# Batch 1's second product as seven Strassen products, and a reordered slot ahead of it

## The chip, the cores and the metric

The kernel runs on one core of one Trainium2 chip. The metric is the device time of one execution in microseconds: median of three runs 208.55 us (208.01 to 209.11). The profile is of one execution with a span of 207.0 us. TensorE multiplies, ScalarE does activations and copies out of PSUM, VectorE does elementwise work and copies, GpSimd copies in SBUF and issues the loads that cast to bf16, SyncE issues stores and DMA transposes.

## The reference, cut to what matters

B = H = 8, S = 512 tokens, NS = 32 states, D = 64; d_model = 512, d_ff = 2048.

```python
scores = x @ state^T / 8 ;  a  = softmax(scores)  ;  xread = a  @ state   # [B,H,512,64]
scores2 = state @ x^T / 8 ; a2 = softmax(scores2) ;  sread = a2 @ x       # [B,H,32,64]
y = concat(xread, sread, axis=2), heads merged to rows                    # [B*544, 512]
out = gelu_exact(y @ w_in) @ w_out                                        # [B*544, 512] f32
```

The first product of the MLP is not taken of xread itself. For each batch the kernel forms P = state x w_in (block-diagonal by head), and then h = a x P, so that attention read and first product are one.

## The kernel before, in words

All work is ordered by hand: each engine runs its instructions in the order in which the Python code issues them, and an instruction that waits holds back everything behind it on its engine or issue queue. Waits follow from data and from buffers. PSUM has four rotating tiles `ps_f` (tag "f") for first products, P chunks, transposes and scores, and four fixed banks `o0` to `o3` for outputs.

Work on a batch b goes through these pieces:

- `load_x(b)` (GpSimd queue, cast to bf16, two buffers), `rearr(b)` (GpSimd copies x into `x4`), `xtr_dma(b)` (SyncE: DMA transpose of `x4` to `xT`), `rearr_ones(b)` (GpSimd copies x into `xo`, with ones beside it for row sums).
- `state_prep` transposes states and sets them into the block-diagonal `sbd`.
- `scores(b, half)` on TensorE, exp on ScalarE (a table load before and after), `norm(b, half)` on VectorE, and `atr_dma(b)` (SyncE: DMA transpose of `a` to `AT`); batches 0 and 1 use TensorE (`atr`) for that.
- `p_mm` makes one of four chunks of P in two PSUM tiles; `p_copy` copies one tile on ScalarE and one on VectorE. `pmat`, `burst` and `p_run` call them, with different PSUM banks.
- `M(k)` is first product number k: batch k // 16, rows m = k % 16 of d_ff; two matmuls of 128x512 into a `ps_f` tile and a Gelu on ScalarE into `gs[b]`. It needs P and AT of its batch. M(32), for example, is the first of batch 2.
- The second product has two forms. In the direct form, `U(u)` (`mm2`) does four matmuls of 128x512 for batch u // 16; sixteen units make a batch (`mm2_m` is the same with another order), and `evac` copies each output tile on VectorE and stores it. In Strassen's form g and w_out are split two by two, and seven products `X(b, "3"), "6", "4", "5", "1", "2", "7"` of 16 matmuls of 128x256 each stand in for the eight of the direct form. They need sums of g blocks (`g_sum`, VectorE), sums of w_out blocks (`w_sums(0)` to `w_sums(4)`, VectorE, once), and combine on VectorE, ScalarE and GpSimd (`u` and `v`).
- `sread`, `sread_out`, `srt` collect the state reads of all batches; their MLP runs at the end (`mm1_sr`, `R`).

In the kernel before, batches 0 and 1 have their second product in the direct form and batches 2 to 7 in Strassen's. The code runs in slots. A slot of batch b in the steady loop (`for b in range(2, B)`, p = 0 to 7) holds M pairs of batch b, the last five products of batch b - 1 (p = 0 to 4: "45127"), and attention and P of batch b + 1; p = 6 and 7 hold X(b, "3") and X(b, "6"). The second slot (M(16) to M(31)) is written out: it holds U12 to U22, and U23 to U31 go into the slot of batch 2. The loads are issued in `load_rest` in the order w_out 1, w_in 2, w_out 2, w_in 3, w_out 3, states of batches 2 to 7, x of batch 2, x of batch 3; x of batch 4 is issued in the second slot. Before a later load, a one-element copy `hold` from a column of g keeps GpSimd's queue back until that Gelu has run.

Of the kernel before, what the change touches and what calls it, by code (L numbers as in the profile page):

```python
# [17 lines left out]
def kernel(  # L18
# [8 lines left out]
    nc = tc.nc  # L27
# [8 lines left out]
    SJ = S // 128  # L36
# [75 lines left out]
    def load_w_out(i):  # L112
        nc.gpsimd.dma_start(out=w_out_bf[:, 4 * i:4 * i + 4, :], in_=w_out_r[:, 4 * i:4 * i + 4, :])
# [18 lines left out]

    def load_rest():
        load_w_out(1)
        for f in range(2, FC):
            load_w_in(512 * f, 512 * f + 512)
            load_w_out(f)
        load_st(2, B)
        load_x(2)
        load_x(3)  # L140


    def keep_warm(n):
# [288 lines left out]

    def burst(chunks, b_read=None):
        done = []
        first = len(chunks) < 4 and b_read is not None
        if first:
            sread(b_read)
        for i, (b, f) in enumerate(chunks):  # L440
            done.append((b, f, p_mm(b, f, ftile if i < 2 else otile)))
        for x in done[:2]:
            p_copy(*x)
        if b_read is not None and not first:
            sread(b_read)
        for x in done[2:3]:
            p_copy(*x)
        if b_read is not None:
            sread_out(b_read)
        for x in done[3:]:  # L450
            p_copy(*x)


    def pmat00(h):
        if h == 0:
            Ps[0] = att.tile([128, 2, d_ff], BF16, name="P", tag="P")
# [42 lines left out]
    def mm2(b, q, j):  # L499
        if q == 0:  # L500
            ops[b, j] = otile([128, d_model], "op")
        ps = ops[b, j]
        for m in range(4 * q, 4 * q + 4):
            nc.tensor.matmul(  # L504
                ps,
                lhsT=gs[b][:, m, j * 128:(j + 1) * 128],
                rhs=w_out_bf[:, m, :],
                start=(m == 0),
                stop=(m == MC - 1),
            )  # L510
        if q == 3:
            rows = out_rows(b, j)
            evac(ps, [(rows, slice(0, 128), 0, d_model)])

    def mm1_sr(m):
        hp = ps_f.tile([128, B * NS], FP32, name="hps", tag="f")
# [276 lines left out]
            nc.vector.tensor_tensor(out=rs["o", 0][:, :NH], in0=ps, in1=rs["u"], op=add)  # L793
            r_out(0)

    def p_run(b, fs, banks):
        done = []
        for f, at in zip(fs, banks):
            it = iter(at or ())
            tiles = (lambda shape, name: otile(shape, name, next(it))) if at else ftile  # L800
            done.append((b, f, p_mm(b, f, tiles)))
        for x in done:
            p_copy(*x)


    def M(*ms):
# [3 lines left out]
    def U(*us):  # L810
        for u in us:
            mm2(u // 16, u % 16 // 4, u % 4)
# [71 lines left out]
    srt(0)  # L884
    U(4, 5)
    rearr_ones(1)
    U(6)
    pmat(0, 2)
    norm(1, 0)
# [4 lines left out]
    sread_out(1)  # L894
    M(10, 11)
    mm2_m(0, 8)
    mm2_m(0, 9)
    burst([(0, 3), (1, 0)])
    mm2_m(0, 10)
    atr(1)  # L900
    M(12, 13)
    srt(1)
    M(14, 15)
    mm2_m(0, 11)
    begin(2)
    rearr(2)
    xtr_dma(2)
    rearr_ones(2)
    U(12)
    burst([(1, 1), (1, 2)])  # L910
    U(13)
    state_prep(2, B)
    M(16, 17)
    U(14)
    M(18, 19)
    U(15)
    burst([(1, 3), (2, 0), (2, 1)])
    U(16)


    u = 17
    for p in range(2, 8):
        if p == 4:
            scores(2, 0)
            scores(2, 1)
            norm(2, 0)
            norm(2, 1)
        if p == 7:
            atr_dma(2)
        if p == 3:  # L930
            begin(3)
            rearr(3)
            xtr_dma(3)
            rearr_ones(3)
        M(16 + 2 * p, 17 + 2 * p)
        U(u)
        u += 1
        if p in (5, 7):
            pmat(2, 2 + p // 7)
        if p >= 3:  # L940
            w_sums(p - 3)
        if p == 2:
            nc.gpsimd.tensor_copy(out=hold, in_=gs[1][:, 4, 0:1])
            load_x(4)

    for b in range(2, B):
        nb = b + 1
        for p in range(8):
            k = 16 * b + 2 * p
            if p == 1 and nb < B:  # L950
                scores(nb, 0)
                scores(nb, 1)
            if p in (2, 3) and nb < B:
                norm(nb, p - 2)
            if p == 3 and nb + 1 < B:
                xtr_dma(nb + 1)
            if p == 5 and nb < B:
                atr_dma(nb)
            if p == 6 and nb < B:
                srt(b)  # L960
            if p == 7 and nb == B - 1:
                srt(nb)
            M(k, k + 1)
            if b == 2:
                for _ in range(2 if p < 4 else 1):
                    if u < 32:
                        U(u)
                        u += 1
            elif p < 5:
                if p == 0:  # L970
                    g_sum(b - 1, "5")
                X(b - 1, "45127"[p])
                if p < 3:
                    g_sum(b - 1, "127"[p])
            if nb == B and p < 4:
                for m in range(4 * p, 4 * p + 4):
                    mm1_sr(m)
            if p == 1 and nb < B:
                sread(b)
                sread_out(b)  # L980
            if p == 4 and nb == B - 1:
                sread(nb)
                sread_out(nb)
            if p == 0 and b + 3 < B:
                nc.gpsimd.tensor_copy(out=hold, in_=gs[b][:, 0, 0:1])  # L985
                load_x(b + 3)
            if p == 0 and nb + 1 < B:
                begin(nb + 1)
                rearr(nb + 1)
            if p == 2 and nb + 1 < B:  # L990
                rearr_ones(nb + 1)
            if nb == B:
                if p == 4:
                    r_homes()
                    r_sum("5")
                    r_sum("2")
                if p == 5:
                    g_sum(b, "6")
                    R("3")
                    r_sum("1")  # L1000
                    R("4")
                    r_sum("6")
                    r_sum("7")
                if p == 6:
# [59 lines left out]
```

The softmax here doesn't subtract the row's maximum and nothing guards it: scores larger than these inputs give would overflow.

## Time and profile before

| what | value |
|---|---|
| median of three runs | 208.55 us |
| span of the profiled run | 207.0 us |
| TensorE granted clock | 1.0 |
| L478 first products (M), 248 matmuls of 128x512 | 63.9 us busy |
| L504 and L531 direct second products, 96 and 32 matmuls of 128x512 | 379 ns each by their records |
| L586 Strassen products, 640 matmuls of 128x256 | 273 ns each by their records |
| L580 sums of g blocks, 30 | 39.8 us busy |
| HBM read and written | 17.30 and 8.91 MB |

Matmul records overlap, since matmuls are pipelined; to price a run of them, the distance between starts is what counts. A busy share says how much an engine works, not what the end waits for: for that the chain of waits and the timelines are read. In timelines the first column is the start and the second the length, both in us; brackets hold idle time and what ended it. "SPq" is SyncE's issue queue.

### The profile page before, as it was taken

To read this page: it belongs to the slowest core of one execution; us is meant where nothing else is said; L and a number is where in the kernel's file an instruction comes from. 1 tells how busy PE (TensorE), PEld (TensorE's weight loads), DVE (VectorE), ACT (ScalarE), POOL (GpSimd) and SP (SyncE) were. 2 spreads that over 40 slices of the span, in tenths; PEclk is the share of its full clock that TensorE was granted. 3 is DMA by queue.
4 is the path that set the end of the run, shared out by engine and by line. 5 is a ranking of instruction groups with operands and counts; after the bars stand their busy time and mean duration, and the time that the engine had idled before them with its cause. 6 is when DMAs were issued, how large, how long until landed. Compare 5 with 4: busy or idle time off the path is not lost.

```text
span 207.0 us, 4716 instructions
## 1 busy us (share of the span) xinstructions
PE 200.9 (97%) x1979; PEld 131.8 (64%) x1979; DVE 138.0 (67%) x219; ACT 133.0 (64%) x240; POOL 62.4 (30%) x69
## 2 busy tenths in 40 slices
PE   7889999998999999999999999999999999999994
PEld 6644444443444567756776677757775788778893
DVE  2942675766919857996599858765878452165883
ACT  3864675679794769576965877587757566744120
POOL 8955400755073005720677005600220002200000
PEclk9999999999999999999999999999999999999999
DMA  6999999689363916827492602560106001030125
GB/s 200 184 168 203 206 198 197 99 237 185 70 80 79 271 29 88 168 103 105 47 175 69 172 0 63 94 203 3 52 3 203 3 0 51 3 152 0 54 92 163
DMA packets 40261, 23.14 MB, mean 112 GB/s; under 512 B 21808, under 2 KB 38320, under 8 KB 40240
## 3 DMA queue, kind: packets, MB, share of 16 engines
q0 software_dynamic: 13936, 8.10, 28.6%
q1 hardware_dynamic: 25616, 14.36, 26.9%
q10 hardware_dynamic: 688, 0.39, 0.6%
q8 instruction: 15, 0.25, 0.5%
q14 instruction: 6, 0.05, 0.1%
HBM read 17.30 MB, written 8.91 MB: 127 GB/s over the span
## 4 chain that ended last, share of the span: by engine, by line
PE 89%; DMA 4%; ACT 3%; POOL 2%; issue 0%; DVE 0%; POOLq 0%; ACTq 0%
PE xp L586 34%; PE hp L478 26%; PE op L504 9%; PE p_ps L415 4%; DMA w_out_bf<-in_moe_w_out_dram 4%; PE op L531 4%; PE hps L518 3%; PE rp L762 3%; PE xp L692 2%; PE pt L324 1%; PE sr L378 1%; POOL w_in_bf L105 1%; POOL sbd L95 1%; ACT g L485 1%; ACT L485 1%; ACT L331 1%
## 5 line engine op out<-in xcount | busy, mean ns | idle before, releaser
L485 ACT ACTIVATE g<-hp 128x512 bf16<-128x512 f32 x124 | 67.5, 604 | 31.0 <-PE hp L478 26.0
L478 PE MATMUL hp<-AT,P 128*128 128x512 bf16 x248 | 63.9, 380 | 0.1
L586 PEld LDWEIGHTS <-gsum 128*128 128x128 bf16 x448 | 43.4, 98 | 11.3 <-issue 2.1
L580 DVE TENSOR_TENSOR gsum<-g 128x2048 bf16<-128x2048 bf16 x30 | 39.8, 1346 | 0.1
L478 PEld LDWEIGHTS <-P 128*128 128x128 bf16 x248 | 22.7, 98 | 19.0 <-issue 1.3
L586 PE MATMUL xp<-ws,gsum 128*128 128x256 bf16 x256 | 30.6, 273 | 0.0
L427 DVE CAST P<-p_ps 128x512 bf16<-128x512 f32 x31 | 20.0, 683 | 13.2 <-PE p_ps L415 13.2
L504 PE MATMUL op<-w_out_bf,g 128*128 128x512 bf16 x96 | 23.7, 379 | 0.0
L586 PE MATMUL xp<-ws,g 128*128 128x256 bf16 x192 | 22.9, 273 | 0.0
L586 PE MATMUL xp<-w_out_bf,gsum 128*128 128x256 bf16 x192 | 22.8, 273 | 0.0
L586 PEld LDWEIGHTS <-g 128*128 128x128 bf16 x192 | 18.8, 98 | 4.3
L426 ACT CAST P<-p_ps 128x512 bf16<-128x512 f32 x31 | 17.0, 605 | 7.0 <-PE p_ps L415 7.0
L635 POOL TENSOR_TENSOR u<-s,oh 128x512 f32<-128x512 f32 x5 | 6.3, 1265 | 48.6 <-ACT oh L632 48.6
L504 PEld LDWEIGHTS <-g 128*128 128x128 bf16 x96 | 9.1, 98 | 11.5 <-issue 1.1
L218 POOL COPY x<-xb 128x1024 bf16<-128x1024 bf16 x12 | 12.6, 1081 | 10.9 <-DMA xb<-in_x_dram 10.9
L228 POOL COPY xo<-xb 128x1024 bf16<-128x1024 bf16 x12 | 14.5, 1241 | 1.3 <-PE sr L378 1.3
L347 DVE TENSOR_TENSOR a<-e,ics 128x512 bf16<-128x512 bf16 x14 | 13.8, 987 | 0.5
L344 DVE TENSOR_REDUCE cs<-e 128x16 f32<-128x512 bf16 x14 | 9.5, 676 | 3.8 <-ACT e L331 3.8
L415 PE MATMUL p_ps<-w_in_bf,sbd 64*32 64x512 bf16 x248 | 10.7, 382 | 0.6 <-ACT g L485 0.5
L605 POOL TENSOR_TENSOR v<-q,oh 128x512 f32<-128x512 f32 x5 | 6.4, 1286 | 14.6 <-ACT oh L637 14.6
L629 DVE TENSOR_TENSOR s<-xp,s 128x512 f32<-128x512 f32 x5 | 3.5, 691 | 11.0 <-PE xp L586 11.0
L985 POOL COPY hold<-g 128x1 bf16<-128x1 bf16 x3 | 1.0, 331 | 31.0 <-ACT g L485 31.0
(111 smaller groups left out, 225.7 us busy)
## 6 DMA issues: line engine op xcount, KB each, us to landing
xb<-in_x_dram POOLq DMA_DIRECT2D x7, 512.0 KB, 7.0
out_dram<-oh SPq DMA_DIRECT2D x13, 256.0 KB, 2.6
out_dram<-osb SPq DMA_DIRECT2D x10, 256.0 KB, 3.3
out_dram<-oh SPq DMA_DIRECT2D x5, 512.0 KB, 2.7
w_out_bf<-in_moe_w_out_dram POOLq DMA_DIRECT2D x4, 512.0 KB, 12.4
w_in_bf<-in_moe_w_in_dram POOLq DMA_DIRECT2D x6, 256.0 KB, 12.6
x0f<-in_x_dram SPq DMA_DIRECT2D x3, 256.0 KB, 3.9
w_in_bf<-in_moe_w_in_dram POOLq DMA_DIRECT2D x4, 128.0 KB, 4.1
```

Of the source, the lines that this page charges most:

```text
L218: nc.gpsimd.tensor_copy(out=A.x4[:, :, :, 64 * t:64 * t + 64].rearrange("p j c d -> p c j d"), in_=src[:, t],)
L228: eng.tensor_copy(out=A.xo[:, :, :, 2 + 64 * t:66 + 64 * t].rearrange("p j c d -> p c j d"), in_=src[:, t],)
L344: nc.vector.reduce_sum(out=cs, in_=e4, axis=AX.X)
L347: nc.vector.tensor_tensor(out=A.a[:, :, hs].rearrange("p g (c n) -> p g c n", n=NS), in0=e4, in1=ics[:, :, :].to_broadcast((128, G, 2, NS) ...
L415: nc.tensor.matmul(ps[t][32 * c:32 * c + 32, :], lhsT=sbd[64 * t:64 * t + 64, b, c, 32 * t:32 * t + 32], rhs=w_in_bf[64 * t:64 * t + 64, c ...
L426: nc.scalar.copy(out=dst[:, 0, :], in_=ps[0])
L427: nc.vector.tensor_copy(out=dst[:, 1, :], in_=ps[1])
L478: nc.tensor.matmul(hp, lhsT=Ps[b][:, t, m * 128:(m + 1) * 128], rhs=atts[b].AT[:, :, t, :], start=(t == 0), stop=(t == 1),)
L485: nc.scalar.activation(out=gs[b][:, m, :], in_=hp, func=AF.Gelu)
L504: nc.tensor.matmul(ps, lhsT=gs[b][:, m, j * 128:(j + 1) * 128], rhs=w_out_bf[:, m, :], start=(m == 0), stop=(m == MC - 1),)
L580: nc.vector.tensor_tensor(out=t, in0=g_q(b, h0, k0), in1=g_q(b, h1, k1), op=op)
L586: nc.tensor.matmul(ps[:, j - js[0], :], lhsT=lhs[:, m, 128 * j:128 * j + 128], rhs=rhs[:, m, :], start=(first and j == js[0] and m == 0), ...
```

## The change

Batch 1 takes Strassen's form too: X(1, "3") and X(1, "6") stand in the second slot and the other five in the slot of batch 2, so the steady loop loses its special case for batch 2. The weight sums, which are now needed a slot earlier, move to the first and second slots. The second slot is reordered: M(16) on come earlier, U12 to U15 of batch 0 later. The state and x of batch 2 are loaded ahead of the last chunk of w_out; x of batch 3 and the states of batches 3 to 7 are loaded in the second slot, behind holds, x of batch 4 and 5 in the slot of batch 2. One chunk of P of batch 1 is copied by VectorE alone, `burst` goes, and the last output tile of batch 0 is stored in two halves. What it is for: fewer matmul columns on TensorE, which is busy nearly all the time, and work that fills the places where TensorE waited.

```diff
     def load_rest():
         load_w_out(1)
-        for f in range(2, FC):
-            load_w_in(512 * f, 512 * f + 512)
-            load_w_out(f)
-        load_st(2, B)
+        load_w_in(1024, 1536)
+        load_w_out(2)
+        load_w_in(1536, 2048)
+        load_st(2, 3)
         load_x(2)
-        load_x(3)
+        load_w_out(3)
...
         if q == 3:
             rows = out_rows(b, j)
-            evac(ps, [(rows, slice(0, 128), 0, d_model)])
+            h = d_model // 2 if j == SJ - 1 else d_model
+            evac(ps, [(rows[:, n:n + h], slice(0, 128), n, n + h) for n in range(0, d_model, h)])
...
+    def p_copy_v(b, f, ps):
+        for t in range(2):
+            nc.vector.tensor_copy(out=Ps[b][:, t, f * 512:(f + 1) * 512], in_=ps[t])
+
+    def hold_for(b, m):
+        nc.gpsimd.tensor_copy(out=hold, in_=gs[b][:, m, 0:1])
...
     rearr_ones(1)
+    w_sums(2)
     U(6)
...
     mm2_m(0, 8)
+    p_run(1, (0, 1), (None, None))
     mm2_m(0, 9)
-    burst([(0, 3), (1, 0)])
+    atr(1)
+    pmat(0, 3)
     mm2_m(0, 10)
-    atr(1)
+    M(16, 17)
+    srt(1)
     M(12, 13)
-    srt(1)
-    M(14, 15)
     mm2_m(0, 11)
     begin(2)
     rearr(2)
     xtr_dma(2)
+    M(14, 15)
+    state_prep(2, 3)
+    pmat(1, 2)
+    hold_for(0, 15)
     rearr_ones(2)
     U(12)
-    burst([(1, 1), (1, 2)])
+    w_sums(0)
+    M(18, 19)
+    hold_for(1, 3)
+    load_x(3)
+    load_st(3, B)
     U(13)
-    state_prep(2, B)
-    M(16, 17)
+    w_sums(1)
+    M(20, 21)
+    scores(2, 0)
+    scores(2, 1)
+    w_sums(3)
     U(14)
-    M(18, 19)
+    p_run(1, (3,), ((3, 0),), p_copy_v)
+    begin(3)
+    rearr(3)
+    xtr_dma(3)
+    rearr_ones(3)
+    M(22, 23)
+    norm(2, 0)
+    M(24, 25)
+    p_run(2, (0,), ((1, 3),))
     U(15)
-    burst([(1, 3), (2, 0), (2, 1)])
-    U(16)
...
-    for p in range(2, 8):
...
-        if p == 7:
-            atr_dma(2)
...
-        M(16 + 2 * p, 17 + 2 * p)
-        U(u)
...
+    norm(2, 1)
+    X(1, "3")
+    atr_dma(2)
+    g_sum(1, "6")
+    M(26, 27)
+    M(28, 29)
+    p_run(2, (1,), ((1, 2),))
+    state_prep(3, B)
+    M(30, 31)
+    X(1, "6")
...
             M(k, k + 1)
-            if b == 2:
-                for _ in range(2 if p < 4 else 1):
-                    if u < 32:
-                        U(u)
-                        u += 1
-            elif p < 5:
+            if b == 2 and p in (0, 3):
+                pmat(2, 2 + p // 3)
+            if b == 2 and p == 1:
+                w_sums(4)
+            if p < 5:
                 if p == 0:
                     g_sum(b - 1, "5")
                 X(b - 1, "45127"[p])
...
             if p == 0 and b + 3 < B:
-                nc.gpsimd.tensor_copy(out=hold, in_=gs[b][:, 0, 0:1])
-                load_x(b + 3)
+                hold_for(b, 0)
+                load_x(4 if b == 2 else b + 3)
+            if p == 6 and b == 2:
+                hold_for(b, 12)
+                load_x(5)
```

More of the change, by code (lines that the diff above doesn't have):

```diff
@@ L430, in pmat @@
         p_copy(b, f, p_mm(b, f, ftile))
[L435 to L451, printed above, removed]
     def pmat00(h):
@@ L794, in R, with p_run @@
             r_out(0)
-    def p_run(b, fs, banks):
+    def p_run(b, fs, banks, copy=None):
         done = []
@@ L802, in p_run @@
         for x in done:
-            p_copy(*x)
+            (copy or p_copy)(*x)
+    def p_copy_v(b, f, ps):
[3 more added lines that the diff above has]
+        nc.gpsimd.tensor_copy(out=hold, in_=gs[b][:, m, 0:1])
     def M(*ms):
@@ L907 @@
     xtr_dma(2)
+    M(14, 15)
+    state_prep(2, 3)
+    pmat(1, 2)
+    hold_for(0, 15)
     rearr_ones(2)
     U(12)
-    burst([(1, 1), (1, 2)])
-    U(13)
-    state_prep(2, B)
-    M(16, 17)
-    U(14)
-    M(18, 19)
-    U(15)
-    burst([(1, 3), (2, 0), (2, 1)])
-    U(16)
-    u = 17
-    for p in range(2, 8):
[L923 to L927, printed above, removed]
-        if p == 7:
-            atr_dma(2)
[L930 to L934, printed above, removed]
-        M(16 + 2 * p, 17 + 2 * p)
-        U(u)
-        u += 1
[L938 to L944, printed above, removed]
+    w_sums(0)
[3 more added lines that the diff above has]
+    load_st(3, B)
+    U(13)
+    w_sums(1)
[3 more added lines that the diff above has]
+    w_sums(3)
+    U(14)
+    p_run(1, (3,), ((3, 0),), p_copy_v)
[7 more added lines that the diff above has]
+    p_run(2, (0,), ((1, 3),))
+    U(15)
+    norm(2, 1)
[8 more added lines that the diff above has]
+    X(1, "6")
     for b in range(2, B):
@@ L963 @@
             M(k, k + 1)
-            if b == 2:
-                for _ in range(2 if p < 4 else 1):
-                    if u < 32:
-                        U(u)
-                        u += 1
-            elif p < 5:
+            if b == 2 and p in (0, 3):
[3 more added lines that the diff above has]
+            if p < 5:
                 if p == 0:
```

## The prediction

> **What bounds the kernel now.** First I read the page's busy shares and its chain of waits.
>
> ```profile
> PE 200.9 (97%) x1979; PEld 131.8 (64%) x1979; DVE 138.0 (67%) x219; ACT 133.0 (64%) x240; POOL 62.4 (30%) x69
> ...
> PE 89%; DMA 4%; ACT 3%; POOL 2%; issue 0%; DVE 0%; POOLq 0%; ACTq 0%
> ```
>
> TensorE is on the chain for 89% of the span; removing matmuls should pay wherever nothing else makes it wait. So next I looked for where it does wait: the timeline of TensorE over the slot that is rearranged (columns: start, length, work).
>
> ```profile
> 47.35 1.03 PE L504 MATMUL op<-w_out_bf,g 128*128 128x512 bf16 x4
> 48.44 1.08 PE L478 MATMUL hp<-AT,P 128*128 128x512 bf16 x4
> 49.36 1.02 PE L504 MATMUL op<-w_out_bf,g 128*128 128x512 bf16 x4
> 50.84 0.89 PE L415 MATMUL p_ps<-w_in_bf,sbd 64*32 64x512 bf16 x8 [0.46 <-ACT g L485]
> 51.82 1.08 PE L478 MATMUL hp<-AT,P 128*128 128x512 bf16 x4
> 52.74 1.02 PE L504 MATMUL op<-w_out_bf,g 128*128 128x512 bf16 x4
> 53.60 1.03 PE L478 MATMUL hp<-AT,P 128*128 128x512 bf16 x4
> 54.46 1.03 PE L504 MATMUL op<-w_out_bf,g 128*128 128x512 bf16 x4
> 55.42 0.41 PE L415 MATMUL p_ps<-w_in_bf,sbd 64*32 64x512 bf16 x8
> 55.76 1.04 PE L478 MATMUL hp<-AT,P 128*128 128x512 bf16 x4
> ```
>
> Lengths overlap; distances between starts count. 52.74 to 54.46 is a first-product pair and a second-product unit: 1.72, so 0.86 each. From 47.35 to 51.82 lie three such and one P chunk (0.34, from 55.42 to 55.76): 2.9 of work in 4.47, so 1.5 us lost, while ScalarE does exp with two table loads. The last line is M(32), the first work on batch 2. It needs AT of batch 2, which comes by a DMA transpose; so last I read SyncE's issue queue, then GpSimd's.
>
> ```profile
> 38.41 2.04 SPq L271 DMA_TRANSPOSE xT<-x  x1
> 40.49 2.46 SPq L493 DMA_DIRECT2D out_dram<-osb  x4
> 47.55 3.12 SPq L271 DMA_TRANSPOSE xT<-x  x1
> 51.80 1.82 SPq L367 DMA_TRANSPOSE AT<-a  x1
> ```
>
> ```profile
> 43.86 0.84 POOL L943 COPY hold<-g 128x1 bf16<-128x1 bf16 x1 [3.50 <-ACT g L485]
> 44.63 0.87 POOL L117 DMA_DIRECT2D xb<-in_x_dram  x1
> 45.50 2.02 POOL L218 COPY x<-xb 128x1024 bf16<-128x1024 bf16 x2
> 47.46 2.02 POOL L228 COPY xo<-xb 128x1024 bf16<-128x1024 bf16 x2
> ```
>
> An xT transpose holds SyncE 2 to 3 us: the stores of batch 0, whose first tile VectorE had ready at 36.4, start at 40.49. AT of batch 2 is issued at 51.80 and lands in 3.1 us, at 54.9: in time for 55.76. The copy for xT of batch 3 starts at 45.50 without waiting, since that x landed long before.
>
> **What the Trainium skill says.** "TensorE: Matmul & The Clock Gate", section "Back-to-back issue gap", gives N/2.4 + 2.5 ns warm: 216 ns for N=512, 109 for N=256. The trace agrees: 0.86/4 = 215 ns; an L586 product of 16 takes 1.75, 109 each. "SBUF — State Buffer", section "Who interferes with whom": a VectorE instruction with two SBUF inputs and a GpSimd one that reads SBUF exclude each other. The trace agrees: two gsum adds beside GpSimd's copies at 79.67 take 3.65, two weight sums alone at 53.39 take 2.35; the hold copy above took 0.84 beside a weight sum, and 0.19 in other slots. The first page's section "What's actually happening" has the clock halve after an idle window of about 3.4 us; no gap of before is that long past the start and the granted clock is 1.0, so no run here shows it.
>
> **The change, part by part.** *Matmuls.* Out go 16 units of 4 (U16 to U31): 16 x 0.865 = 13.8. In come 7 products of 1.75: 12.25. Net -1.6 us on TensorE; this is all that Strassen's form itself saves; the 1.5 us of waits above could come on top.
>
> *VectorE, ScalarE, GpSimd.* Batch 1's output loses four 0.69 evacuation copies on VectorE and gains four 0.69 adds, so these cancel; new are five gsum adds of 1.22 (+6.1 us of VectorE), three 0.58 copies on ScalarE and the u and v of GpSimd (1.26 each). The weight sums only move. By the table of busy time per stretch VectorE is busy 3.9 of 5 us at 38 to 43 and 1.65 of 5 at 43 to 48; with the sums, one P chunk copied wholly on it (2 x 0.64) and two norms (1.65 each) set there, it is continuously busy from about 38 to 50, and ends norm(2,1) near 50. w_sums(2), set early, fills a gap of 1.34 that VectorE has at 24: free.
>
> *Loads.* w_out chunks land one per 2.6 us before (22.2, 27.2, 32.3; x of batch 2 at 36.3). Moving a 32 KB state and x ahead gives x2 at 32.8 and the last w_out at 35.4; its first user, U12, stands near 37. Free. State of batches 3 on then lands behind x3, just ahead of its transposes. Splitting the store of batch 0's last tile in two is one more SyncE issue; a store's issue takes 0.39 (L600) to 0.6 (2.46 for the four above).
>
> *TensorE's new order.* I added up starts by hand from 22.18 (identical to there): 12 units, 12 pairs, 2 products, seven P chunks (2.6), scores 0.47, small ones 1.35: 28.7, so M(32) could start at 50.9. I then set the waits. P of batch 1 comes one unit earlier than before, while sread_out still holds a PSUM tile until 29.75: 0.6 lost. The next single chunk waits for a Gelu: 0.25. Scores(2) puts table, exp, table into ScalarE from 41.4 to 45.1 (2 x 1.28 + 1.08, as before), but U14, P, two pairs and U15 stand there with free tiles: about 0.2. gsum6 behind norm(2,1) delays X(1,"6") by 0.3. With 0.2 for the small gaps at changes of shape, TensorE reaches M(32) at 52.5.
>
> *The new wait.* x3 is now loaded late: load_x(3) stands on GpSimd behind rearr_ones(2), itself behind a hold on Gelu 15, and a hold on Gelu 19. M(8) to the unit after it end at 29.2, as before; P with its wait to 30.4; then three units, M(16,17), M(12,13), atr 0.45, P 0.34, srt and small gaps 0.2: M(14,15) runs 35.6 to 36.5, and 0.16 for the matmul's tail and 0.6 for the Gelu give Gelu 15 at 37.3. State transposes 0.1, P with its wait 0.6, U12 and M(18,19) 0.87 each, the tails again: Gelu 19 at 39.8. AT of batch 2 stands on SyncE behind xT of batch 3, which needs x3. Step by step:
> - rearr_ones(2), two copies 2.02, up to 2.48 against w_sums(0): ends 40.2;
> - hold 0.19 and gap 0.33 (hold up to 0.84): load starts 40.7;
> - landing 6.1 as for the load at 44.63 (5.6 to 7.0 later): 46.8;
> - rearr(3) 2.02 to 2.48: 48.9;
> - xT on SyncE 2.04 (1.92 to 3.12, the long ones while an x load is in flight, not so here): 51.0;
> - two half stores, 0.45 each (0.39 to 0.6), whose data VectorE has ready at 48: 51.9;
> - AT 3.5 (3.1 to 4.9): 55.4.
>
> So M(32) starts at 55.4, not 52.5: TensorE stands 2.9 us, and every instruction on it is queued behind. Taking all small ends gives 53.2, and three or four of the large ends 57.
>
> *Batch 2's slot.* Before, M(32) at 55.76 to X(2,"3") at 71.23 is 15.47. Nine units (7.8) go; five products (8.75) and two P chunks (0.7) come: 17.1. w_sums(4) joins the adds; gsum2 and gsum7 still come just ahead of X2 and X7. But x4 is now issued at M(32)+2, not at 44.6, so rearr(4), u, rearr_ones(4), v run late on GpSimd, and v ends about when P of batch 3 wants the banks that the adds after v release: I take 0.3 (0 to 0.8). From X(2,"3") on, the code is the same.
>
> *Sum.* X(2,"3") at 55.4 + 17.1 + 0.3 = 72.8 against 71.2: +1.5 us; 208.55 becomes **210.0**. The break-even for M(32) is 71.23 - 17.1 - 0.3 = 53.8.
>
> **The rivals.** *A, only the matmuls count:* x3, or AT, arrives by 52.5, so TensorE sets the pace: 52.5 + 17.1 = 69.6, -1.6, **206.9**. For it: TensorE's 89% of the chain, the scarce waits before. Against: even the smallest value at each step of the x3 chain gives 53.2. It takes an error in where Gelu 15 and 19 fall, of over a microsecond.
> *B, it cancels:* the chain runs at its smallest values, M(32) at 53.2 to 54.3: 53.7 + 17.1 + 0.1 = 70.9, **208.3**. For it: 5.6 us landings and 1.92 us transposes both occur. Against: they don't come together with quiet copies, VectorE being full of two-input sums then.
> *C, the lock and the clock:* w_sums against rearr_ones and hold costs 1.2 (as the 0.84 hold shows in kind), M(32) at 56.8, and an idle stretch near 4 us halves the clock for a while: +3.3, **211.9**. For it: VectorE has no gaps there. Against: GpSimd waits more than it works.
>
> **How the numbers follow.** Forecast 0.55, A 0.15, B 0.20, C 0.10. The likeliest is 210.0. The lower end stands at A's time, 207.0, leaving about half of A below; the upper, 211.6, leaves C's upper part. 0.5% is 1.04 us: slower than 209.6 is most of the forecast (0.47) and C (0.10): 0.57. Within: the rest of it (0.08) and most of B (0.17): 0.25. Faster: A and the end of B: 0.18.
>
> **What the changed profile would show.** L568, the products' new line, with 16 x 7 more matmuls; M(32) (L459) at 55 to 56 with a gap ahead of it that ends on the AT transpose, not on ScalarE; SyncE's xT of batch 3 at about 49, two half stores, AT at about 52; load of x3 at about 40.7 on GpSimd; the gap at 47 to 52 gone; 17.1 us from M(32) to X(2,"3"). It is wrong if TensorE's first batch-2 matmul stands before 53.8 or if the next slot is shorter than 16.8.

## The result and the profile after

The change made the kernel slower: 214.64 us (median of 4 runs, 213.96 to 215.28) against 208.34 us (4 runs, 208.01 to 209.11), ratio 1.029 [1.025, 1.033]. The forecast was 210.0 with a range to 211.6: the side was right, the size was not. One version below, number 16, has two of its six executions in a slower state: its median and ratio are of the other four, its profile of one of the two.

First the page of after, the busy shares and the chain of waits:

```profile
PE 201.8 (95%) x2027; PEld 137.1 (65%) x2027; DVE 146.5 (69%) x227; ACT 133.8 (63%) x242; POOL 71.1 (33%) x74
...
PE 74%; POOL 11%; DMA 5%; issue 4%; DVE 3%; SPq 1%; ACT 1%; POOLq 0%; DVEq 0%; ACTq 0%
```

TensorE's share of the chain fell from 89 to 74%, and GpSimd's rose from 2 to 11%: now the end waits for copies and loads. TensorE's busy time even rose by 0.9 us, though 1.6 us of matmuls went. The timeline of TensorE (start, length, work) shows where:

```profile
49.00 1.03 PE L459 MATMUL hp<-AT,P 128*128 128x512 bf16 x4
51.27 1.92 PE L568 MATMUL xp<-ws,gsum 128*128 128x256 bf16 x16 [1.25 <-DVE gsum L562]
55.76 1.04 PE L459 MATMUL hp<-AT,P 128*128 128x512 bf16 x4 [2.56 <-DMA AT<-a]
56.72 0.41 PE L415 MATMUL p_ps<-w_in_bf,sbd 64*32 64x512 bf16 x8
57.06 3.45 PE L568 MATMUL xp<-ws,g 128*128 128x256 bf16 x16
60.31 0.80 PE L324 MATMUL pt<-sbd,xT 128*128 128x64 bf16 x16
```

X(1, "6") waits 1.25 for a sum on VectorE; M(32) waits 2.56 for the DMA transpose of batch 2's softmax; and X(1, "4") behind it takes 3.25 from its start to the next instruction, where 16 such matmuls take 1.75. The table by stretch says why; its column PEclk is the granted clock:

```profile
core 0: us, PE busy (x) PEld busy (x) DVE busy (x) ACT busy (x) POOL busy (x), PEclk, DMA share, GB/s
55.00:57.00 2.00, 1.24 (x12) 0.42 (x12) 0.00 (x0) 0.54 (x2) 0.00 (x0) 1.00 0.06 11
57.00:57.25 0.25, 0.25 (x10) 0.18 (x3) 0.02 (x1) 0.25 (x2) 0.07 (x1) 1.00 0.00 0
57.25:58.00 0.75, 0.75 (x6) 0.52 (x5) 0.75 (x2) 0.75 (x2) 0.47 (x2) 0.50 0.00 0
58.00:60.00 2.00, 2.00 (x11) 1.45 (x10) 1.05 (x1) 1.30 (x2) 0.53 (x1) 0.50 0.38 21
60.67:61.00 0.33, 0.33 (x15) 0.33 (x13) 0.33 (x1) 0.09 (x1) 0.00 (x0) 1.00 1.45 195
```

From 57.25 to 60.67 the clock is half. GpSimd's timeline and SyncE's queue show where AT comes from:

```profile
38.81 0.71 POOL L792 COPY hold<-g 128x1 bf16<-128x1 bf16 x1 [0.41 <-ACT g L466]
39.46 0.89 POOL L117 DMA_DIRECT2D xb<-in_x_dram  x1
...
46.67 2.02 POOL L218 COPY x<-xb 128x1024 bf16<-128x1024 bf16 x2 [5.38 <-DMA xb<-in_x_dram]
48.63 3.49 POOL L228 COPY xo<-xb 128x1024 bf16<-128x1024 bf16 x2
```

```profile
48.72 2.71 SPq L271 DMA_TRANSPOSE xT<-x  x1
51.53 1.00 SPq L474 DMA_DIRECT2D out_dram<-osb  x2
52.64 1.24 SPq L367 DMA_TRANSPOSE AT<-a  x1
```

This is the chain that the prediction described: hold, load of x3 (39.46, landed 46.62), copy, xT of batch 3, two half stores, and only then AT of batch 2, landed at 55.71. VectorE had finished `a` at 49.2: AT lay 3.4 us in the queue, behind the next batch's transpose and two stores.

Profiled executions start up to a microsecond or so apart, so they are compared by distances. I use four: M(8), which stands ahead of nearly all that was moved, to M(32); M(32) to X(2, "3"); X(2, "3") to the last VectorE add; and the tail, from the end of that add (0.29) to the end of the span.

| version | M(8) to M(32) | M(32) to X(2,"3") | to last add | tail | median |
|---|---|---|---|---|---|
| before | 29.69 | 15.47 | 132.86 | 2.6 | 208.34 |
| after | 30.64 | 19.72 | 132.72 | 3.7 | 214.64 |
| difference | +0.95 | +4.25 | -0.14 | +1.1 | +6.3 |

The differences add to 6.15, the medians differ by 6.3. (The two profiled executions differ by 5.2, since after's reached M(8) 0.95 earlier.) So the loss lies in three places: 0.95 until M(32), 4.25 in batch 2's slot, and 1.1 behind the last add, where no code was changed.

### The profile page after: what moved, and what is told of

Same layout as the page of the kernel before. It is cut to its first block, busy times and chain, and to the rows that moved or that the text cites. A ratio compares the mean times of both kernels' runs of the same rounds, so it can differ in the third digit from the quotient of the medians.

```text
span 212.2 us, 4831 instructions
## 1 busy us (share of the span) xinstructions
PE 201.8 (95%) x2027; PEld 137.1 (65%) x2027; DVE 146.5 (69%) x227; ACT 133.8 (63%) x242; POOL 71.1 (33%) x74
## 4 chain that ended last, share of the span: by engine, by line
PE 74%; POOL 11%; DMA 5%; issue 4%; DVE 3%; SPq 1%; ACT 1%; POOLq 0%; DVEq 0%; ACTq 0%
PE xp L568 33%; PE hp L459 20%; PE p_ps L415 4%; DMA xb<-in_x_dram 3%; PE hps L500 3%; PE op L513 3%; PE rp L744 3%; POOL x L218 2%; POOL xo L228 2%; POOL w_in_bf L105 2%; PE op L485 2%; PE xp L674 2%; DMA AT<-a 1%; PE pt L324 1%; PE sr L378 1%
## 5 line engine op out<-in xcount | busy, mean ns | idle before, releaser
L568 PEld LDWEIGHTS <-gsum 128*128 128x128 bf16 x528 | 51.1, 98 | 14.8 <-issue 2.3
L562 DVE TENSOR_TENSOR gsum<-g 128x2048 bf16<-128x2048 bf16 x35 | 47.2, 1365 | 0.1
L568 PE MATMUL xp<-ws,gsum 128*128 128x256 bf16 x304 | 36.4, 273 | 1.2 <-DVE gsum L562 1.2
L568 PE MATMUL xp<-ws,g 128*128 128x256 bf16 x224 | 28.3, 282 | 0.0
L568 PE MATMUL xp<-w_out_bf,gsum 128*128 128x256 bf16 x224 | 26.6, 273 | 0.0
L568 PEld LDWEIGHTS <-g 128*128 128x128 bf16 x224 | 22.5, 101 | 5.7 <-issue 0.2
L228 POOL COPY xo<-xb 128x1024 bf16<-128x1024 bf16 x12 | 18.0, 1530 | 0.0
L587 POOL TENSOR_TENSOR v<-q,oh 128x512 f32<-128x512 f32 x6 | 8.4, 1394 | 13.5 <-ACT oh L619 13.5
L590 DVE TENSOR_TENSOR oh<-xp,v 128x512 f32<-128x512 f32 x6 | 4.1, 689 | 8.6 <-POOL v L587 8.6
L415 PEld LDWEIGHTS <-sbd 64*32 64x32 bf16 x248 | 3.2, 89 | 9.9 <-issue 9.1
```

The lines of the kernel that those rows point to most:

```text
L228: eng.tensor_copy(out=A.xo[:, :, :, 2 + 64 * t:66 + 64 * t].rearrange("p j c d -> p c j d"), in_=src[:, t],)
L415: nc.tensor.matmul(ps[t][32 * c:32 * c + 32, :], lhsT=sbd[64 * t:64 * t + 64, b, c, 32 * t:32 * t + 32], rhs=w_in_bf[64 * t:64 * t + 64, c ...
L562: nc.vector.tensor_tensor(out=t, in0=g_q(b, h0, k0), in1=g_q(b, h1, k1), op=op)
L568: nc.tensor.matmul(ps[:, j - js[0], :], lhsT=lhs[:, m, 128 * j:128 * j + 128], rhs=rhs[:, m, :], start=(first and j == js[0] and m == 0), ...
L587: nc.gpsimd.tensor_tensor(out=xs[b, "v"], in0=xs[b, "q"], in1=o[:, :, :NH], op=ALU.subtract)
```

## The experiments

The versions are edits of after unless said; each was timed beside before.

**1. AT of batch 2 ahead of xT of batch 3 on SyncE.** It takes away the queue in front of AT, not the late load.

```diff
     rearr(3)
-    xtr_dma(3)
     rearr_ones(3)
...
     atr_dma(2)
+    xtr_dma(3)
```

> The changed kernel with one instruction moved: SyncE's transpose of xT of batch 3 stands behind the transpose of AT of batch 2, nothing else. Theory 1 (TensorE's 2.56 us at M(32) come from AT of batch 2 queued on SyncE behind xT of batch 3, which waits for x of batch 3; the half clock after it follows from that stand): AT is issued at 49.3, when norm(2,1) ends, and lands at 52.5; M(32) follows X(1,6) at 53.0, the clock stays at 1.0 afterwards, and the time is 4.6 us below 214.6: about 210. Theory 2 (the extra sums and adds of the products hold VectorE and GpSimd, and TensorE waits for them one way or another): the wait moves to another instruction, under 1 us is gained: about 214.

```profile
50.53 1.88 SPq L367 DMA_TRANSPOSE AT<-a  x1
```

```profile
52.50 1.92 PE L568 MATMUL xp<-ws,gsum 128*128 128x256 bf16 x16 [1.23 <-DVE gsum L562]
54.26 1.03 PE L459 MATMUL hp<-AT,P 128*128 128x512 bf16 x4
```

Measured 211.38, ratio 1.015 [1.009, 1.020], where after has 1.029: about 3 us of 6.3 come back. SyncE issues AT at 50.53, as soon as VectorE's norm is done, and M(32) stands directly behind X(1, "6") at 54.26. M(8) to M(32) is 27.90, 2.74 less than in after and 1.79 less than in before: without the queue the reordered slot does save what it was made for. The slot is 18.67 at full clock, still 1.3 over the forecast's 17.4: P of batch 3 waits twice (0.32 and 0.22 by the records), and from the M pair ahead of it to X(2, "3") 3.80 pass, 2.44 before.

**2. x3 and the states loaded right behind the last w_out chunk,** both loads and the hold for Gelu 19 out of the slot. Now xT of batch 3 is early and the order on SyncE stays.

```diff
         load_w_out(3)
+        load_x(3)
+        load_st(3, B)
...
-    hold_for(1, 3)
-    load_x(3)
-    load_st(3, B)
```

> The changed kernel with x of batch 3 and the states of batches 3 to 7 loaded right behind the last w_out chunk instead of behind the hold on Gelu 19; SyncE's order stays. Theory 1: rearr(3) follows rearr_ones(2) at about 38.5 on GpSimd, xT of batch 3 leaves SyncE by 46, AT of batch 2 is issued at 49.3 and M(32) stands at 53.0, so again about 210. Theory 2: under 1 us gained. If GpSimd's copies at 38 to 42 slow the weight sums beside them, norm(2,1) ends up to 1 us later and about 211 remains.

Measured 210.98, ratio 1.014 [1.009, 1.018]; M(8) to M(32) 28.41, and no half clock. So cutting the chain at its other end gives much the same: 2.23 us until M(32), where version 1 gives 2.74. A new wait came: the two weight sums took 3.42 instead of 2.34 beside GpSimd's copies, and P waited 0.38 and 0.23 behind them at 44.

**3. The stand filled, to part the clock from the wait:** 40 dummy matmuls of 128x128 on zeros between X(1, "6") and M(32).

```diff
     X(1, "6")
+    keep_warm(40, 1)
```

> The changed kernel with 40 dummy matmuls of 128x128 on zeros between X(1,6) and M(32), which fill 2.3 us of TensorE's stand; they change nothing that is computed. Theory 1's second half (the product after M(32) takes 3.25 instead of 1.75 us because the stand lets the clock fall to half): M(32) stays near 55.8, the granted clock stays at 1.0, X(1,4) takes 1.75, and 1.9 us are gained: about 212.7. Rival (X(1,4) is slow from its operands or its bank, not from the clock): no gain, 214.6.

```profile
53.29 2.40 PE L146 MATMUL warm_ps<-warm 128*128 128x128 bf16 x40
55.61 1.02 PE L459 MATMUL hp<-AT,P 128*128 128x512 bf16 x4
...
56.91 1.92 PE L568 MATMUL xp<-ws,g 128*128 128x256 bf16 x16
```

Measured 212.67, ratio 1.020 [1.016, 1.024]; X(1, "4") takes 1.75 again. The time agrees with the expectation, but partly by luck, and the distances say so: M(32) came 0.66 earlier by itself, the slot shrank from 19.72 to 18.78 (0.94), and the tail by 0.9, to 2.8. The half clock cost 1.67 in place (1.50 on X(1, "4"), 0.17 on the scores behind it) but counts 0.94 net. P of batch 3 waits for a bank that comes free behind GpSimd's v, and v ends 16.14 behind M(32) here, 17.08 in after, so only 0.94 earlier; P now waits 0.68 and 0.22.

**4. Strassen's form alone, in the old order,** an edit of before: the reordering left out.

```diff
-    U(16)
...
-        U(u)
-        u += 1
+        if p == 4:
+            X(1, "3")
+        if p == 6:
+            g_sum(1, "6")
+            X(1, "6")
...
```

> The kernel before with Strassen's form for batch 1 alone: the loads, the first slot and the holds stay as before; U16 to U31 go, X(1,3) stands behind M(24,25), X(1,6) behind M(28,29), the other five in the slot of batch 2 as in the changed kernel. Theory 1 (the form pays, the reorder's transposes cost): ScalarE sets the pace of the second slot, M(32) at about 52.5, and the slot of batch 2 takes 16.4 us, so X(2,3) at about 69 against 71.2 and the time 206 to 207. Theory 2 (the form itself costs VectorE and GpSimd time that TensorE waits for): not below 208.3.

Measured 216.25, ratio 1.038 [1.033, 1.042]: of the two theories the first failed, and the second, that TensorE waits for VectorE's part of the form, is what the trace shows.

```profile
55.44 3.60 PE L586 MATMUL xp<-ws,gsum 128*128 128x256 bf16 x16 [3.87 <-DVE gsum L580]
```

The sum for X(1, "6") stands on VectorE behind two norms (the product of the first takes 2.16 for 0.69 beside GpSimd's copies), two weight sums and a P copy, and TensorE stands 3.87 us, then works at half clock. So "the form pays, the order costs" is wrong: placed so, the form brings VectorE work that the old order has no room for. Other places for the two products in the old order were not tried, so that it takes this reorder is not shown.

**5. Loads alone,** an edit of before: x2, then the last w_out chunk, the states, and x3.

> The kernel before with the new order of loads alone: state and x of batch 2 ahead of the last w_out chunk, then the states of batches 3 to 7 and x of batch 3 right behind it; order of work and direct second product of batch 1 unchanged. The prediction costs the loads at nothing (U12, first user of the last w_out chunk, stands near 37, and the chunk lands at 35.4): 208.3, within 0.5 of before. Rival: the loads matter: with x of batch 2 3.5 us earlier its copies on GpSimd meet other VectorE work, or w_out is late: over 209; or a gain, below 207.5, if SyncE's transposes of batch 2 held up something.

Measured 209.01, ratio 1.002 [1.001, 1.004]; M(8) to M(32) 30.16, slot 15.47. Nearly free: 0.4 us, within the 0.5 expected. Until M(32) it loses 0.47, of which 0.31 is a wait of U12 for the last w_out chunk, at 34.97; in after U12 stands later and has no such wait.

**6. Version 1 with `rearr_ones(3)` placed behind X(1, "6")** in the code.

> As the run with AT ahead of xT, and rearr_ones(3), two GpSimd copies that stood beside norm(2,1) and gsum6, moved behind X(1,6) in the program. Theory L (VectorE's adds with two SBUF inputs and GpSimd's copies shut each other out): norm(2,1)'s product takes 0.69 instead of 1.38 or little more, gsum6 1.22 instead of 2.05, the wait of 1.23 us ahead of X(1,6) shrinks below 0.3, and 1 us or so is gained: about 210.3 against 211.4. Rival (VectorE simply has too much work ahead of gsum6): the wait stays over 1 us and the time at 211.4. Either way the wait on the adds behind v in the slot of batch 2 stays at about 1.1 us, or grows, since GpSimd's copies now stand nearer to it.

Measured 210.50, ratio 1.012 [1.009, 1.015]. The edit did nothing: no GpSimd work lay between the two places, the copy ran right behind `rearr(3)` as before (48.88, 3.49) and the sum for X(1, "6") again took 2.06. So its theory is not tested here. It is a repeat of version 1, and the two ratios agree within their intervals. The medians differ by 0.9 (211.38 and 210.50), but so do those of the kernel before beside them, 208.86 and 208.10: it is ratios that can be compared between versions.

**7. Version 1 with x4 loaded early,** behind the states, to end the waits of batch 3's P.

```diff
     load_st(3, B)
+    load_x(4)
...
-                load_x(4 if b == 2 else b + 3)
-            if p == 6 and b == 2:
-                hold_for(b, 12)
-                load_x(5)
+                load_x(b + 3)
```

> As the run with AT ahead of xT, and x of batch 4 loaded behind the states of batches 3 to 7 in the second slot, x of batch 5 at the start of the slot of batch 2 as in the kernel before. Theory P (P of batch 3 waits 1.1 us for its banks because x of batch 4 lands at about 62, and rearr(4), u, rearr_ones(4) and v follow it on GpSimd): rearr(4) starts right behind Gelu 32, v ends before 66, the two P chunks take 0.6 us instead of 1.7, and 1.1 us is gained: about 210.3 against 211.4. Rival (the chunks wait for VectorE, which has more adds in that slot): no gain.

Measured 213.12, ratio 1.024 [1.021, 1.028]: worse than version 1. VectorE's and GpSimd's timelines lie side by side:

```profile
56.06 3.85 DVE L562 TENSOR_TENSOR gsum<-g 128x2048 bf16<-128x2048 bf16 x1
```

```profile
56.79 2.03 POOL L218 COPY x<-xb 128x1024 bf16<-128x1024 bf16 x2
```

The copies of x4 now fall on the sum for X(1, "5"), 1.22 us alone, 3.85 here; TensorE stands 1.43 for it. The AT transpose, with x4's load in flight, lands after 4.9 us, and M(32) waits 1.05.

**8 and 9. All waits at once:** x3, the states and x4 early, AT first; and then the first P pair one unit later.

> The changed kernel with all that was found: x of batch 3 and the states loaded behind the last w_out chunk, x of batch 4 behind rearr_ones(2), AT of batch 2 ahead of xT of batch 3 on SyncE, rearr_ones(3) behind X(1,6). If late loads, SyncE's order and the copies beside VectorE are the whole of the excess: gsum6 is ready when M(31) ends, M(32) stands about 1.6 us earlier than with x of batch 3 early alone, P of batch 3 doesn't wait: 211.0 - 1.6 - 1.1 = 208.3, level with the kernel before. If something of Strassen's form in itself costs: 210 or more.

> As the run with all waits mended, and the first slot's P chunks of batch 1 one unit later (behind mm2_m(0,9), as in the kernel before), with the units of m = 10 and 11 set behind the chunk pair and behind the chunk of batch 0. The chunk pair took 0.88 us instead of 0.56 since it waits for the PSUM tile that sread_out frees. Expected: that wait goes, 0.3 to 0.6 us gained on the run with all waits mended, 207.8 to 208.0; if M(12,13) then crowds ScalarE behind M(16,17), nothing or a loss of up to 0.5.

Measured 216.42 (1.039 [1.036, 1.042]) and 216.25 (1.037 [1.033, 1.040]), where 208.3 and 207.8 to 208.0 were expected: both expectations failed. GpSimd's copies of x2 and x3 now run from 36.4 to 43.6 through the two weight sums, which take 5.77 instead of 2.34; P waits 2.80 for a PSUM tile behind them, and the clock halves there too. Moving the P pair cured that pair and nothing else.

**10. Version 1 with `w_sums(1)` and `w_sums(3)` moved** behind the sum for X(1, "6"), just ahead of M(30, 31): less work on VectorE ahead of batch 2's norms and that sum.

> As the run with AT ahead of xT, and w_sums(1) and w_sums(3), 2.34 us of VectorE between U13 and U14, moved behind gsum6 and the state copies, where VectorE stood 1.8 us; they are needed by X(1,4) and X(1,1), both later. Theory V (VectorE's queue ahead of norm(2,1) and gsum6 holds X(1,6) and AT of batch 2): norm(2,1) ends 2 us earlier, X(1,6) follows M(31) without its wait of 1.1 to 1.2 us, M(32) follows it at 52.1 instead of 53.3, and about 1.1 us is gained on the 210.9 that the two runs with this SyncE order have as their mean: 209.8. Rival (what holds VectorE is GpSimd's copies of x of batch 3, at 46.9 to 52.4, whatever stands beside them): gsum6 or the moved sums stretch instead, X(1,4) waits for its sum, and the time stays at 210.5 to 211.5.

Measured 210.11, ratio 1.010 [1.008, 1.012]. The second norm's product now ends before GpSimd's copies start and takes 0.69 again; the sum still takes 2.06 beside them, but X(1, "6") waits no more. Yet M(32) waits 1.01: AT, issued at 47.52, while the load of the states was ending, landed only 5.1 us later.

**11. Version 10 with x4 early and its copies on ScalarE.**

> As the run with the sums later, and x of batch 4 loaded in the second slot with its two copies for xT made by ScalarE (p = 2 and 3 of batch 2's slot) instead of GpSimd. With x of batch 4 early but copied by GpSimd, the chunks of P of batch 3 no longer waited, but gsum5 took 3.85 us beside the copies. If the exclusion of GpSimd's copies and VectorE's adds is what stood in the way, gsum5 takes 1.22 here, P of batch 3 takes 0.6 instead of 1.7, and 1.1 us more is gained: 208.7 if the run before gives 209.8. If ScalarE's copies hold up Gelus instead, a wait on them appears ahead of a first product at p = 3 or 4 and the gain is under 0.5.

Measured 215.02, ratio 1.033 [1.031, 1.036]. The sum for X(1, "5") takes 1.22 where it took 3.85 in version 7, now that no GpSimd copy runs beside it, and P of batch 3 no longer waits (M pair to X(2, "3") 2.45, as before), so the theory of those waits holds. But AT of batch 2, issued with x4's load in flight, landed 7.1 us later: M(32) waits 2.99, the clock halves. And xT of batch 4, now made later, starts on SyncE only at 72.61 (66.56 in after), still ahead of AT of batch 3, and M(48) waits 1.78.

**12. Version 10 with the states loaded behind the last w_out chunk,** and `rearr_ones(4)` behind v.

```diff
         load_w_out(3)
+        load_st(3, B)
...
     load_x(3)
-    load_st(3, B)
...
-            if p == 2 and nb + 1 < B:
+            if p == (4 if b == 2 else 2) and nb + 1 < B:
                 rearr_ones(nb + 1)
```

> Edit on the version with the two weight sums moved behind gsum6: the states of batches 3 to 7 are loaded right behind the last w_out chunk instead of behind x of batch 3, and rearr_ones of batch 4 goes behind v in batch 2's slot. In that version AT of batch 2 was issued at 47.52 and landed 5.1 us later, while the states' load (7.9 us from 40.41) was just ending, and P of batch 3 waited 0.32 and 0.23 for adds behind v, which stands on GpSimd behind a 3.0 us copy. Theory D (waits are what is left, each costs its length): AT lands in 3.2 to 3.5 us, M(32) starts behind X(1,6) at about 51.6, not 52.6, and the pair of P chunks of batch 3 takes 0.6, not 1.3: 210.1 - 1.0 - 0.7 = 208.4, level with the kernel before. Rival E (the transfer of AT is slow for another cause, the xT transpose of batch 3 queued right behind it): AT again lands after 4.5 to 5 us and only the P part is gained: 209.4. Rival F (waits move, as in the two versions with x of batch 4 loaded early): the copies of rearr_ones meet other VectorE adds and stretch them, 210 or more.

Measured 209.29, ratio 1.004 [1.002, 1.006].

```profile
51.95 1.04 PE L460 MATMUL hp<-AT,P 128*128 128x512 bf16 x4 [0.20 <-DMA AT<-a]
```

AT, issued at 47.62, landed 4.3 us later, not the 3.2 to 3.5 expected, but in time for all but 0.2 (in version 13, with the same work here, it landed 3.1 us later); M(8) to M(32) is 26.64, the shortest so far. P of batch 3 shows no wait in the timeline, yet M pair to X(2, "3") still takes 3.19 for 2.45: the pair was paced in small pieces, and this half of the expectation failed. M(8) to the last add is 177.48, 0.5 *less* than before's 178.02. Still the kernel is 0.7 slower. What is left is the tail.

**13 to 17. The tail.** The tail was defined above: from the end of the last VectorE add to the end of the span. Up to here before, version 5 and version 3 had tails of 2.6 to 2.8, all others 3.7 to 4.1. These have 1979, 1979 and 2067 TensorE matmuls; the others 2027 (in some profiles a few records of them are missing). Version 13 is version 12 with 17 wide warming matmuls for 55 narrow ones at the start (1989); 14 is version 12 with 15 dummies more in a stand near 10 us (2042); 15 is version 12 without the split store; 16 is after with the 15 dummies; 17 is *before* with 48 dummies more (2027).

> The version with the states loaded early, its 55 warming matmuls of 128x128 on zeros at the start replaced by 17 of 128x512 (which compute nothing of the result either): 38 matmuls fewer, 1989, near the 1979 of the kernel before. It is about the tail: from the last VectorE add to the end of the span the kernel before, its version with the loads alone (1979 matmuls) and the version with 40 dummy matmuls (2067) take 2.6 to 2.8 us, all ten others (2027 or a few more) 3.7 to 4.1, with unchanged code there. Theory T: the tail depends on the number of TensorE instructions ahead of it: 2.6 to 2.8 here, time 209.3 - 1.0 = 208.2. Rival: it depends on the work or the stores ahead of it: 3.7 again, 209.3. If the wider warming matmuls change the start, the distance from M(8) to the last add shows the rest: 177.5 in that version.

> The version with the states loaded early, with 15 more dummy matmuls in a stretch near 10 us where TensorE stands for 1.06 us (27 there for 12), so at no cost of their own. Theory T (the tail goes by the number of TensorE instructions, long at 2027, short at 1979 and 2067): 2042 lies between, so the tail may be either; if short, 208.2. Rival (stores or work set it): 3.7, 209.3.

> The version with the states loaded early, with the last output tile of batch 0 stored in one piece, as in the kernel before: the one part of the change not tried alone. Theory: a second issue costs 0.5 us on SyncE just ahead of AT of batch 2, which is issued at 47.6 only when VectorE's norm is done, so nothing is gained on TensorE: same as that version, 209.3, and its tail stays 3.7. Rival S: one store fewer makes the tail 2.7: 208.2.

> The kernel after with the same 15 dummy matmuls more near 10 us, 2042 instead of 2027. Ledger: the tail falls from 3.7 to 2.7 and nothing else changes (M(8) to the last add 183.1): 214.6 - 1.1 = 213.5. Rival: the tail's cure belongs to the version with the states loaded early, 214.6.

> The kernel before with 48 dummy matmuls more near 10 us (60 for 12), which makes 2027 TensorE matmuls, as many as the kernel after has; they also hold the start up, by some 48 x 0.055 - 0.5 = 2.1 us, which the distance from M(8) leaves out. If 2027 is what makes the tail long, whatever the work: tail 3.7 us instead of 2.6, M(8) to the last add 178.0 as before, time 208.6 + 2.1 + 1.1 = 211.8. Rival: the long tail needs the changed program too: tail 2.6, 210.7.

| version | matmuls | M(8) to last add | tail | median | ratio to before |
|---|---|---|---|---|---|
| 12 | 2027 | 177.48 | 3.7 | 209.29 | 1.004 [1.002, 1.006] |
| 13, fewer | 1989 | 177.48 | 2.6 | 208.12 | 0.998 [0.996, 0.999] |
| 14, more | 2042 | 177.50 | 2.7 | 208.14 | 0.997 [0.995, 0.999] |
| 15, one store | 2027 | 177.96 | 3.9 | 209.33 | 1.004 [1.003, 1.006] |
| 16, after | 2042 | 182.44 | 3.8 | 212.80 | 1.020 [1.016, 1.025] |
| 17, before | 2027 | 178.01 | 3.7 | 210.81 | 1.010 [1.008, 1.012] |

The end of SyncE's queue, of before, then of version 17, then of version 13 (the last three stores):

```profile
202.64 1.83 SPq L651 DMA_DIRECT2D out_dram<-oh  x3
```

```profile
203.73 2.69 SPq L651 DMA_DIRECT2D out_dram<-oh  x3
```

```profile
201.65 1.83 SPq L634 DMA_DIRECT2D out_dram<-oh  x3
```

Version 17 has before's schedule to the hundredth (178.01 for 178.02) and after's tail; versions 13 and 14 have version 12's schedule and before's tail. So in these the tail goes with the number of TensorE instructions, not with the schedule, and (version 15) not with the split store.

The DMA packets of the traces say more. The pages of before and of after list, among the DMA queues:

```profile
q8 instruction: 15, 0.25, 0.5%
```

```profile
q8 instruction: 16, 0.26, 0.5%
```

This queue moves packets of 16 KB all through the run. In the thirteen traces of the kernels above with a long tail, version 16 apart, its last packet starts 0.06 to 0.40 us before the last add ends, while the last stores are under way; in the five with a short tail it starts 3.5 us or more before that end. The later the packet ends, the longer the tail: an end 0.5 to 0.6 us behind that of the add goes with tails of 3.7, 0.8 with 3.9, and 0.9 with 4.0 to 4.1. In before, the first of the last three stores lands 2.3 us after its issue, in after 3.9. Versions 13, 14 and 17 move packet and tail together and leave the schedule alone. How a packet holds up a store no run shows. Version 16 is the exception: its packet starts 3.45 us before that end, yet the tail is 3.8. But in that execution the clock was half from 10.8 to 14.2 as well, the packet took 1.5 us, and the store ahead of the last three held SyncE for 1.41, 0.56 in after. Its ratio, 1.020 against after's 1.029, is a fall of 1.9 us where 1.1 was expected, from executions spread between 211.5 and 214.3; so there the cure is not shown.

Versions 13 and 14 beat both kernels, before by 0.5 us.

## Why the prediction was wrong, point by point

The step that failed most is the price of batch 2's slot: 17.1 + 0.3 forecast, 19.72 measured. Two terms of it were too small. The half clock was put at nothing, behind a stand that the prediction itself put at 2.9 us; it counts 0.94 net. The wait of P of batch 3, put at 0.3, is about 1.4 where the clock stays full, and the slot then still takes 18.67 (version 1) and 18.78 (version 3). The chain ahead of M(32), 1.3 too short, and the tail, taken at nothing and 1.1 longer, are the other two misses.

- *What bounds the kernel, and the new wait:* right in kind. The gap ahead of M(32) ends on AT; the chain through hold, x3, copy, xT, stores and AT is in the profile; versions 1 and 2 cut it at either end and get 2.2 to 2.7 us back until M(32).
- *The chain's lengths: low by 1.3.* M(32) was forecast 0.36 ahead of before's and came 0.95 behind. The load started 0.3 earlier than forecast; landing took 7.2, not 6.1 (+1.1); xT held SyncE 2.71, not 2.04 (+0.7), although no x load was in flight; stores and gaps +0.3; AT landed in 3.07, not 3.5 (-0.4). All single values lay in or near the ranges given; that xT would be short because no x load is in flight was the reason that failed.
- *The matmuls, -1.6:* right. From M(32) to batch 3's M pair version 1 needs 14.87; before's 13.03 - 7.8 + 8.75 + 0.7 makes 14.7.
- *The half clock, put at nothing in the slot's sum: +1.67 in place, 0.94 net by version 3.* It was given to rival C alone, at 0.10, for "an idle stretch near 4 us", and C's sum leaves 0.3 for it (56.8 + 17.1 + 0.3 is 3.0 above before, and C says 3.3). The Trainium skill's page "TensorE: Matmul & The Clock Gate", section "What's actually happening", says the clock halves after an idle window of about 3.4 us, and that such windows run freely. The prediction read it as a stand of 3.4. In all traces the stretches between two changes of the clock are whole multiples of 3.41 us, which agrees with such windows; but an idle one is not needed. The window ahead of after's half clock, 53.84 to 57.25, holds 1.92 us of the 2.56 stand and 1.49 us of work. Over all traces, windows with 2.09 us or more without a matmul record were followed by a half clock and those with 1.75 or less were not; between, both occur. An estimate from these lengths: a stand of 2.9 us puts 1.92 or more into one window for seven of ten places where the windows can lie, one of 2.56 for six of ten. So the forecast's own stand should have carried the halving as likely, not as certain. One of after's four executions had a mean clock of 1.0, the others 0.989 to 0.992; its span was 212.4 against 212.2 to 213.5, so single runs don't resolve the cost.
- *P of batch 3, taken at 0.3 (0 to 0.8): 0.74 in after, about 1.4 where the clock stays full* (M pair to X(2, "3") 3.80 in version 1 and 3.91 in version 3, 2.44 before). With u and v at 1.26 and copies at 2.02, as the prediction quotes them, rearr(4), u, `rearr_ones(4)` and v make 6.6; in after they take 3.1, 1.7, 3.0 and 1.7, that is 9.5, beside VectorE's two-input work. The lock of the Trainium skill's page "SBUF — State Buffer", section "Who interferes with whom", which I used for GpSimd's copies in the second slot only, was missed here; in version 11, where x4 comes early and rearr(4) leaves GpSimd, the wait is gone.
- *The wait of X(1, "6") for norm(2,1) and its sum, taken at 0.3:* 1.25. The norm's product took 1.38 for 0.69 and the sum 2.06 for 1.22 beside GpSimd's copies. In after this hides behind the wait for AT; in version 1 it doesn't.
- *Loads free:* nearly, 0.4 (version 5).
- *The tail, 1.1:* taken at nothing ("From X(2,"3") on, the code is the same"). Nothing in the profile of before told it.

The sum: 210.0 + 1.3 (chain) + 1.7 (clock) + 0.4 (P) + 0.2 (rest of the slot) + 1.1 (tail) - 0.1 = 214.6; that it closes so well has 0.2 of luck in it, since 210.0 was counted from 208.55 and before measured 208.34 beside after. The rivals: A's and B's place for M(32) needed a chain that ran at its smallest values; it ran above its middle ones. C was the nearest, but in part by luck. Its M(32) at 56.8 was met (56.7, counted from M(8)), though not by its cause: it charged 1.2 to the lock ahead of x3's load, and that load started 0.3 earlier than forecast. Its half clock came, at five times the price.

## What to carry to other kernels

On an in-order DMA queue, ask of each transfer who waits for it next: a transpose for the next batch ahead of one for this batch cost 2.7 us up to its first matmul, and moving one line gave it back. When a stand of some 2 us or more is forecast on TensorE, count a halved clock with it as a chance, by how much of the stand can fall into one 3.41 us window. Elementwise work with two inputs that moves beside GpSimd copies must be priced at its stretched length on both engines, and a kernel that is retimed by half a per cent should be measured with a few dummy instructions more and fewer, since the program's length alone moved the end by 1.1 us. The place of the last packet of the queue "instruction" against the last stores told long tails from short ones in all traces here but one.

## What the runs showed of the hardware that was not expected

- The tail: 2.6 to 2.7 us with 1979, 1989 and 2042 TensorE matmuls and 3.7 with 2027, on schedules otherwise unchanged (versions 12 to 14; before and 17). In eighteen of nineteen traces it is long exactly when the last 16 KB packet of the queue "instruction" falls among the last stores; version 16 has a long tail without that.
- The half clock came in stretches of 3.41 us after stands of 2.09 (version 16), 2.56 (after), 2.80 (version 8), 2.97 (version 9) and 2.99 us (version 11), and of twice that round the stand of 3.87 (version 4); after one of 1.78 (version 11) and shorter ones later than the kernel's start it did not. In after it begins 1.5 us after work resumed, in version 8 at once: it follows a window, not the stand.
- A VectorE sum of 128x2048 took 1.22 alone and 1.7 to 3.85 beside GpSimd copies, a pair of weight sums 2.34, 3.42 and 5.77; in version 7 the copies were hardly slowed (2.03), in after they took up to 3.5.
- The DMA transpose of `a` landed 3.1 to 5.0 us after its issue with no GpSimd load in flight: 3.1 to 3.8 in most versions, 4.3 and 4.7 in 12 and 15, which have the same work there as 13 (3.1), 4.6 and 5.0 in 8 and 9. With a load in flight or just ending it took 4.9 (version 7), 5.1 (version 10) and 7.1 us (version 11). So only the 7.1 stands out; that the load is its cause was not tried by itself.
